# Gates' quotient by VectorE's reciprocal in place of ScalarE's exponential, with a reordered front and rows turned by PE transposes

## The chip, the core and the metric

The kernel runs on one core of a Trainium2 chip. Its engines are TensorE (PE; its weight loads are PEld), VectorE (DVE), ScalarE (ACT) and GpSimd (POOL); SyncE (SP) issues most of the DMAs. Each engine works through its own list of instructions in order and waits on semaphores for the others. The metric is the time of one execution on the device in microseconds (us).

## The reference

A linear recurrence with complex gates ("gate loop") feeds a mixture of experts that picks one expert for each token.

```
q, k, v, a_re, a_im: (B=4, H=8, S=768, D=48) float32
mag   = sqrt(a_re^2 + a_im^2)
scale = min(mag, 0.999) / (mag + 1e-6)
a     = (a_re + i a_im) * scale
for t in range(S):
    S_state = a[t][:, None] * S_state + outer(k[t], v[t])     # complex; k v is real
    y[t]    = q[t] @ Re(S_state)
x      = y as rows: (B*S = 3072 tokens, H*D = 384)
logits = x @ w_gate + modality_bias[modality_id]              # 8 experts
e      = argmax(logits);  g = softmax(logits)[e]
out    = g * (relu(x @ w1[e]) @ w2[e])                        # F = 1024
```

## The kernel before

**Units and groups.** The 768 steps are cut into G = 6 chunks of L = 128 steps. A unit is one chunk of one batch entry, all 8 heads: 24 units, in the order `order` (chunk by chunk, four batch entries each). Gates are worked out for NG = 2 units at once: 12 groups x. Steps lie on the 128 partitions; a group's gates are 2 x 8 x 48 = 768 elements a partition.

**Gates.** In a chunk the products of the gates become sums: of log magnitudes and of angles, each a product with a triangular matrix on PE. For a group x:

- `load_a` (L127) brings a_re and a_im into `abs_`, which has two places, used in turn (x % 2); `load_qk` (L136) brings q and k, also two places.
- `squares` (L143): ACT squares both, DVE adds: half 1 of `sq` is |a|^2, half 0 is a_re^2.
- `products` (L156): on DVE, `tan` = a_re * a_im and `neg` = (a_re < 0).
- `logs` (L165): ACT takes the logarithm of both halves, 1536 elements.
- `tangents` (L170): ACT's exponential of minus the logarithm of a_re^2 is 1 / a_re^2; a second one gives `off`, the correction for the 1e-6. DVE clamps the log magnitude (`lm`) and multiplies `tan` by 1 / a_re^2, so that it holds a_im / a_re.
- `arctans` (L183), `angles` (L186): ACT's arctangent, then PE sums over the steps into `u` (L197, L198).
- `carries`, `fractions` (L201, L210): add the angle at the end of the last chunk (through DRAM, `f_scr`, L207 and L226) and take the fraction of a turn. `waves` (L230): sine and cosine on ACT into `css`.
- `sums`, `moduli` (L238, L248): PE sums the log magnitudes into `ls`, ACT's exponential gives the moduli and their inverses, `pm`; the chunk's last row goes through DRAM (`m_scr`, L256), and `decays` (L259) reads it back.

Logarithm and exponential lie in one of ACT's table sets (EXP), arctangent and sine in another (TRIG); `table` (L116) loads a set, and `then` (L111) keeps ACT's activations in the order in which they are written.

**A unit's own stages.** `hats` (L269) multiplies q and k with moduli and waves on DVE (L279, L283); `turned` (L292) transposes them on PE (L307) and copies them on ACT (L308); `inner` (L315) forms the masked products inside half-chunks and the state's updates (PE L326 and L336, DVE L327, L341 to L348); `outer` (L352) forms y transposed (PE L360 and L366) and copies it to `yT` on ACT (L367): 4 blocks of 128 partitions (two heads of 48, each padded to 64) by 128 steps. `rows` (L370) turns `yT` back, steps on the partitions, and forms the logits in the same products: the right side, `sel`, holds for each block an identity (48 columns) and the router's weights (8 columns). There are 8 products of 64 rows into 56 columns (L377). ACT copies 384 columns as the token's row (L388), DVE adds the 8 partial logits (L389).

**Order.** L411 to L437 write the front: loads of the first groups, then the gates of groups 0 and 1. The loop (L441) then runs half a period a turn: at an even w the fractions, sums and moduli of later groups and their logarithms (under EXP), at an odd w arctangents, waves and squares (under TRIG); each turn carries one unit through `turned`, `inner`, `outer` and `rows`. A planner orders the instructions of PE, DVE and POOL from this text by when it expects their inputs; `issue_after` and `add_manual_dep` hold single ones back. SP's DMAs wait in their queue, one behind the other. `dense` (L88) gives PE extra products whose results nobody reads, at places where it would idle.

**After the gates.** A router (class `Router`, fed by `lg`, with a reciprocal of 4 or 8 elements a partition at L639) places the tokens by expert in DRAM (scatter, L668), and `Layers` runs the experts' products (L951, L966) from there. The first two sets of weights reuse the memory of `abs_` and `css`.

## Time and profile before

| what | before |
|---|---|
| runs (3): lowest, median, highest | 362.83, 366.56, 367.34 us |
| the profiled execution: time, span | 367.03, 365.4 us |
| mean granted clock of TensorE | 0.888 |
| bytes moved in all | 43.04 MB |
| table loads on ACT | 25, 1283 ns each |

The profile is of one execution. Its span runs from the first to the last instruction. A group's row gives its busy time and the mean duration of one instruction; the durations of neighbours on an engine overlap a little, so that busy time in a stretch is less than the sum of durations. The page also has the chain of waits: from the last instruction back, at each step to what released it.

### The profile page before, as it was taken

What the parts mean: (1) busy time and instruction counts of PE and PEld (TensorE: products, weight loads), DVE (VectorE), ACT (ScalarE), POOL (GpSimd) and SP (SyncE); (2) the same over time, 40 slices, a digit from 0 to 9 for tenths busy, and PEclk for the clock granted to TensorE, in tenths of its full rate; (3) what the DMA queues carried; (4) which work ended last, traced back from release to release, by engine and by line L of the source; (5) the groups of instructions that cost most, each with busy time, mean ns of one, the idle gap of its engine ahead of it and who ended that gap; (6) DMA issues with size and microseconds to landing.
All of it is one profiled execution on the core that took longest, in us unless ns stands there. A gap on an engine that the chain in (4) does not pass through costs nothing.

```text
span 365.4 us, 11564 instructions
## 1 busy us (share of the span) xinstructions
PE 322.6 (88%) x4954; PEld 248.9 (68%) x4954; DVE 242.4 (66%) x443; ACT 240.6 (66%) x289; POOL 65.0 (18%) x91
## 2 busy tenths in 40 slices
PE   2786998999899999787999999599989779999992
PEld 1334676587878787756778889489878547777761
DVE  2669799998999899755788899013242733465440
ACT  3987999999999997945689865023113337555532
POOL 7000000000000000072000004710130523424323
PEclk9898999899999999986799999755655969999998
DMA  8967877988766678981968411292120543323221
GB/s 154 209 137 161 170 127 136 173 191 163 134 144 120 138 72 155 180 194 43 167 121 148 88 24 36 75 174 50 30 59 0 148 137 111 108 92 125 85 83 51
DMA packets 155282, 43.04 MB, mean 118 GB/s; under 512 B 145602, under 2 KB 151494, under 8 KB 155096
## 3 DMA queue, kind: packets, MB, share of 16 engines
q1 hardware_dynamic: 149592, 31.98, 45.3%
q0 software_dynamic: 5632, 10.25, 10.7%
q8 instruction: 41, 0.67, 0.7%
q14 instruction: 17, 0.14, 0.1%
HBM read 38.00 MB, written 9.15 MB: 129 GB/s over the span
## 4 chain that ended last, share of the span: by engine, by line
PE 56%; ACT 19%; issue 6%; DMA 6%; SPq 6%; DVE 3%; another core or an unknown queue 2%; POOL 1%; POOLq 0%; DVEq 0%; ACTq 0%
PE h_ps L951 8%; PE y_ps L966 7%; PE up L336 6%; PE xw L377 6%; PE yp L366 5%; PE wp L326 4%; ACT sq L120 4%; PE u L197 4%; ACT L117 3%; PE ls L243 3%; ACT pm L120 3%; PE yp L360 3%; PE tKT L307 2%; DMA qk<-in_k_dram 2%; DMA abs<-in_a_im_dram 2%
## 5 line engine op out<-in xcount | busy, mean ns | idle before, releaser
L336 PE MATMUL up<-V,QK 64*96 64x48 f32 x704 | 41.6, 256 | 3.8 <-issue 2.7
L668 POOL DMA_INDIRECT x_rows<-packed,place x24 | 29.1, 1215 | 86.4 <-DVE U L346 40.2
L336 PEld LDWEIGHTS up<-V,QK 64*96 64x96 f32 x704 | 38.1, 170 | 6.1 <-issue 2.9
L283 DVE TENSOR_TENSOR QK<-css,qkp 128x1536 f32<-128x1536 f32 x24 | 42.0, 1751 | 0.2
L966 PE MATMUL y_ps<-w2t,hT 128*128 128x384 bf16 x200 | 37.2, 340 | 5.3 <-issue 2.8
L367 ACT COPY yT<-yp 128x512 f32<-128x512 f32 x24 | 14.0, 583 | 41.2 <-PE yp L366 33.1
L951 PE MATMUL h_ps<-xgT,w1t 128*128 128x256 bf16 (+1 forms) x312 | 37.7, 281 | 0.0
L951 PEld LDWEIGHTS <-w1t 128*128 128x128 bf16 x312 | 31.0, 103 | 6.1 <-issue 0.3
L377 PE MATMUL xw<-sel,yT 64*128 64x56 f32 x384 | 32.2, 313 | 1.1 <-ACT QT L308 0.6
L117 ACT ACT_TABLE_LOAD x25 | 32.1, 1283 | 1.4 <-PEq L1071 0.9
L971 POOL DMA_INDIRECT out_dram<-y_sb,xg x25 | 24.9, 994 | 44.6 <-ACT y_sb L969 40.7
L326 PEld LDWEIGHTS wp<-QT,KT 96*64 96x64 f32 x768 | 26.5, 148 | 9.0 <-ACT yT L367 2.7
L966 PEld LDWEIGHTS <-hT 128*128 128x128 bf16 x200 | 19.3, 101 | 19.0 <-issue 5.3
L326 PE MATMUL wp<-QT,KT 96*64 96x64 f32 x768 | 29.9, 236 | 2.3 <-ACT yT L367 2.0
L377 PEld LDWEIGHTS xw<-sel,yT 64*128 64x128 f32 x384 | 28.7, 221 | 3.6 <-ACT QT L308 0.7
L308 ACT COPY KT<-tKT 96x1024 f32<-96x1024 f32 x24 | 24.2, 1007 | 10.6 <-PE tKT L307 10.5
L867 POOL DMA_DIRECT2D abs<-in_moe_w_dram x2 | 1.8, 901 | 160.5 <-DMA qk<-in_k_dram 146.2
L389 DVE TENSOR_REDUCE lg<-xw 128x8 f32<-128x64 f32 x24 | 5.3, 220 | 35.6 <-ACT packed L388 35.6
L969 ACT ACTIVATE y_sb<-y_ps,xg 128x384 f32<-128x384 f32 x25 | 13.2, 577 | 23.4 <-PE y_ps L966 17.0
L197 PE MATMUL u<-tan,turn 128*128 128x384 f32 x48 | 21.9, 541 | 4.3 <-ACT yT L367 2.4
L308 ACT COPY QT<-tQT 96x1024 f32<-96x1024 f32 x24 | 24.3, 1014 | 1.2 <-PE tQT L307 1.2
L954 ACT ACTIVATE hT<-h_ps 128x1024 bf16<-128x1024 f32 (+1 forms) x17 | 17.0, 998 | 11.9 <-remote 6.4
(198 smaller groups left out, 631.6 us busy)
## 6 DMA issues: line engine op xcount, KB each, us to landing
abs<-in_a_re_dram SPq DMA_DIRECT2D x24, 192.0 KB
abs<-in_a_im_dram SPq DMA_DIRECT2D x24, 192.0 KB
qk<-in_q_dram SPq DMA_DIRECT2D x24, 192.0 KB
qk<-in_k_dram SPq DMA_DIRECT2D x24, 192.0 KB
V<-in_v_dram SPq DMA_DIRECT2D x24, 192.0 KB
cb<-f_scr SPq DMA_DIRECT2D x10, 384.0 KB
xg<-x_rows SPq DMA_DIRECT2D x12, 194.0 KB
x_rows<-x_rows SPq DMA_DIRECT2D x8, 194.0 KB
```

The costliest lines, as they stand in the source:

```text
L117: then(nc.scalar.preload_act_table_set(name))
L120: then(nc.scalar.activation(*args, **kw))
L197: nc.tensor.matmul(us[:, i], turn[:], tan[:, i], start=True, stop=False)
L283: box["hat"] = nc.vector.tensor_tensor(QK[:].rearrange("p a h c d -> p a (h c d)"), wave, twice, Alu.mult)
L308: nc.scalar.copy(to[:], tp)
L326: nc.tensor.matmul(wp[rows_, h, :], KT[:, s, h], QT[:, s, h], start=True, stop=True)
L336: ins = nc.tensor.matmul(up[:, s, h], flat[rows_, h * C:(h + 1) * C], V[rows_, h, 0:D], start=True, stop=True)
L377: ins = nc.tensor.matmul(xw[:, u, j], yT[at_u, j], sel[at_u, j], start=True, stop=True)
L668: put = self.put = nc.gpsimd.indirect_dma_start(out=self.x_rows, out_offset=bass.IndirectOffsetOnAxis(ap=place[:, i:i + 1], axis=0), in_=p ...
L951: nc.tensor.matmul(h_ps[:, f // nf, f % nf, :], w1t[:, k, ff * 128:(ff + 1) * 128], xgT[:, k, :], start=(k == 0), stop=(k == KD - 1))
L966: nc.tensor.matmul(y_both[:, s], self.hT[:, f, s * 128:(s + 1) * 128], w2t[:, f, :], start=(f == 0), stop=(f == NF - 1))
L971: sc = self.sc = nc.gpsimd.indirect_dma_start(out=self.out, out_offset=bass.IndirectOffsetOnAxis(ap=xg[:, Dt // 2 + 1:], axis=0), in_=y_sb ...
```

## The change

It has three parts. First, `products` takes the reciprocal of a_re on DVE and multiplies it by a_im, which gives the quotient at once; `logs` then takes only half 1, and `tangents` loses its first exponential and its product on DVE. In the loop the quotient of x+4 moves from the end of an odd turn (x+5 there) to the start of an even one, and the load of x+6 behind it. Second, the front starts under TRIG: quotients, arctangents, angles and sines of the first groups come ahead of any logarithm, and the logarithms of group 1 go into the loop's first turn; the loads of `sel` go behind those of the second q and k, the cast of `identb` goes to POOL, and some counts and data of `dense` differ. Third, `rows` turns `yT` by 4 PE transposes of 128x128 against `ident` and forms the logits by 4 accumulated products with 8 columns; `sel` keeps the weights alone, and DVE copies the logits instead of adding them.

```diff
--- before
+++ after
@@ -141,8 +141,8 @@
         box["qk", x] = qk
 
     def squares(x):
-        ab = box.pop(("ab", x))
-        if x in (1, 2):
+        ab = box["ab", x]
+        if x == 1:
             sq = css[:, 1].rearrange("p i h c d -> p (i h c d)").rearrange("p (a i h d) -> p a i h d", a=2, i=NG, h=H)
         else:
             sq = el.tile([L, 2, NG, H, D], F32, name="sq", bufs=1)
@@ -151,33 +151,34 @@
         ins = nc.vector.tensor_tensor(sq[:, 1], sq[:, 0], sq[:, 1], Alu.add)
         if x > 6:
             tc.add_manual_dep(ins.ins, box["hat"].ins.name, mybir.DependencyInfo(mybir.DependencyClass.NoSync, mybir.DependencyReason.DATA), reason="behind the products that the transposes wait for")
-        box["squares", x] = sq, ab
+        box["squares", x] = sq
 
     def products(x):
 
-        ab = box["squares", x][1]
+        ab = box["ab", x]
         tan = el.tile([L, NG, H, D], F32, name="tan", bufs=2)
-        nc.vector.tensor_tensor(tan[:], ab[:, 0], ab[:, 1], Alu.mult)
         neg = el.tile([L, NG, H, D], BF16, name="neg", bufs=2)
-        nc.vector.tensor_scalar(neg[:], ab[:, 0], 0.0, None, Alu.is_lt)
-        box["products", x] = tan, neg
+        if x == 0:
+            nc.vector.tensor_scalar(neg[:], ab[:, 0], 0.0, None, Alu.is_lt)
+        nc.vector.reciprocal(tan[:], ab[:, 0])
+        nc.vector.tensor_tensor(tan[:], tan[:], ab[:, 1], Alu.mult)
+        if x:
+            nc.vector.tensor_scalar(neg[:], ab[:, 0], 0.0, None, Alu.is_lt)
+        box["tangents", x] = tan, neg
 
     def logs(x):
 
-        sq = box["squares", x][0]
-        act(sq[:], sq[:], Act.Ln)
+        sq = box["squares", x]
+        act(sq[:, 1], sq[:, 1], Act.Ln)
 
     def tangents(x):
 
 
-        sq, (tan, neg) = box.pop(("squares", x))[0], box.pop(("products", x))
-        act(sq[:, 0], sq[:, 0], Act.Exp, scale=-1.0)
+        sq = box.pop(("squares", x))
         off = el.tile([L, NG, H, D], BF16, name="off", bufs=2)
         act(off[:], sq[:, 1], Act.Exp, scale=-0.5, bias=ln_eps[:])
         lm = el.tile([L, NG, H, D], F32, name="lm", bufs=3)
         nc.vector.tensor_scalar(lm[:], sq[:, 1], 2.0 * math.log(0.999), None, Alu.min)
-        nc.vector.tensor_tensor(tan[:], tan[:], sq[:, 0], Alu.mult)
-        box["tangents", x] = tan, neg
         box["lm", x] = lm, off
 
     def arctans(x):
@@ -189,8 +190,7 @@
         us = pair([L, H, D], "u")
         full = box["full"][:, 0]
         if x == 0:
-            for n, data in ((18, neg), (11, box["lm", 0][1]), (6, box["lm", 1][1])):
-                dense(full, n, data[:, 0].rearrange("p h d -> p (h d)"))
+            dense(full, 10, neg[:, 0].rearrange("p h d -> p (h d)"))
         elif x == 2:
             dense(full, 5)
         for i in range(NG):
@@ -239,6 +239,8 @@
 
         lm, off = box.pop(("lm", x))
         ls = pair([L, H, D], "ls")
+        if x == 0:
+            dense(box["full"][:, 0], 14)
         for i in range(NG):
             nc.tensor.matmul(ls[:, i], half[:], lm[:, i], start=True, stop=False)
             ins = nc.tensor.matmul(ls[:, i], nhalfb[:], off[:, i], start=False, stop=True)
@@ -299,7 +301,7 @@
             full = box["full"][:, 0]
             if i == 0 and u == 0:
                 dense(full, 10)
-                dense(full, 5, box["pm", 0][:, 1, 0].rearrange("p h d -> p (h d)"))
+                dense(full, 4, box["pm", 0][:, 1, 0].rearrange("p h d -> p (h d)"))
             elif i == 0:
                 dense(full, FILLED.get(u, 0))
             for h in range(H):
@@ -370,11 +372,13 @@
     def rows(g, b):
 
         yT = box.pop(("outer", g, b))
-        xw = pair([L, J, D + Router.E], "xw")
+        xw = pair([L, 512], "xw")
+        xt = xw[:, 0].rearrange("t (j c) -> t j c", c=L)
+        logits = xw[:, 1, 0:Router.E]
         for j in range(J):
-            for u in range(2):
-                at_u = slice(u * 64, (u + 1) * 64)
-                ins = nc.tensor.matmul(xw[:, u, j], yT[at_u, j], sel[at_u, j], start=True, stop=True)
+            nc.tensor.transpose(xt[:, j], yT[:, j], ident[:])
+        for j in range(J):
+            ins = nc.tensor.matmul(logits, yT[:, j], sel[:, j], start=j == 0, stop=j == J - 1)
         busy.append(ins)
         m = g * B + b
         m0 = max(c for c in takes.values() if c <= m)
@@ -385,8 +389,8 @@
             box["packed"] = packed
         packed = box["packed"]
         xr = packed[:, m - m0, 0:H * D // 2].bitcast(BF16)
-        nc.scalar.copy(xr.rearrange("t (j u d) -> t u j d", u=2, d=D), xw[:, :, :, 0:D])
-        nc.vector.tensor_reduce(lg[:, m, :], xw[:, :, :, D:].rearrange("t u j e -> t e u j"), axis=AX.XY, op=Alu.add)
+        nc.scalar.copy(xr.rearrange("t (j u d) -> t j u d", u=2, d=D), xt.rearrange("t j (u c) -> t j u c", u=2)[:, :, :, 0:D])
+        nc.vector.tensor_copy(lg[:, m, :], logits)
 
     NX = len(groups)
     NU = len(order)
@@ -411,29 +415,25 @@
     for x in range(2):
         phase(load_a, x)
     phase(load_qk, 0)
+    table(TRIG)
+    phase(products, 0)
+    phase(squares, 0)
+    phase(load_a, 2)
+    phase(arctans, 0)
+    phase(angles, 0)
+    phase(products, 1)
+    phase(squares, 1)
+    phase(load_a, 3)
+    phase(arctans, 1)
+    phase(angles, 1)
+    phase(fractions, 0)
+    phase(waves, 0)
     table(EXP)
-    phase(squares, 0)
-    phase(products, 0)
-    phase(load_a, 2)
     phase(logs, 0)
-    phase(squares, 1)
     phase(tangents, 0)
-    phase(products, 1)
-    phase(load_a, 3)
-    for x in range(2):
-        phase(logs, x)
-        phase(tangents, x)
-    table(TRIG)
-    for x in range(2):
-        phase(arctans, x)
-        phase(angles, x)
-    phase(fractions, 0)
     phase(squares, 2)
-    phase(squares, 3)
-    with tc.issue_after(box["last"].ins):
-        phase(products, 2)
-    phase(waves, 0)
     phase(load_qk, 1)
+    load_sel()
     phase(fractions, 1)
 
     rt = None
@@ -448,23 +448,28 @@
         unit(values, n + 2)
         unit(values, n + 3)
         if even:
-            phase(load_a, x + 6)
             phase(carries, x + 4)
             phase(fractions, x + 3)
+            with tc.issue_after(box["hat" if w > -4 else "last"].ins) if w < 0 else nullcontext():
+                phase(products, x + 4)
+            phase(load_a, x + 6)
         else:
             phase(load_qk, x + 3)
             phase(decays, x + 2)
-            hats(n + 3)
             if w == -3:
                 hats(0)
+            hats(n + 3)
             if w > 3:
                 hats(n + 4)
         unit(turned, n + 2)
         if even:
-            if x + 2 < NX:
+            if -4 < w and x + 2 < NX:
                 table(EXP)
             phase(sums, x + 2)
             phase(moduli, x + 2)
+            if w == -4:
+                phase(logs, 1)
+                phase(tangents, 1)
             phase(logs, x + 4)
         elif x + 3 < NX:
             table(TRIG)
@@ -481,7 +486,6 @@
         else:
             phase(waves, x + 3)
             phase(squares, x + 5)
-            phase(products, x + 5)
         if w == NU:
             layers.turn(0)
         unit(rows, n - 1)
@@ -1040,17 +1044,18 @@
     ident = cpool.tile([128, 128], F32, name="ident")
     make_identity(nc, ident[:])
     identb = cpool.tile([128, 128], BF16, name="identb")
-    nc.vector.tensor_copy(identb[:], ident[:])
+    nc.gpsimd.tensor_copy(identb[:], ident[:])
     lg = cpool.tile([128, N // 128, E], F32, name="lg")
 
-    sel = cpool.tile([128, H // 2, D + E], F32, name="sel")
+    sel = cpool.tile([128, H // 2, E], F32, name="sel")
     nc.gpsimd.memset(sel[:], 0.0)
-    for u in range(2):
-        nc.gpsimd.tensor_copy(sel[u * 64:u * 64 + D, :, 0:D], ident[u * 64:u * 64 + D, None, u * 64:u * 64 + D].broadcast_to([D, H // 2, D]))
-        nc.sync.dma_start(out=sel[u * 64:u * 64 + D, :, D:], in_=moe_w_gate.rearrange("(j u d) e -> u d j e", u=2, d=D)[u])
+
+    def load_sel():
+        for u in range(2):
+            nc.sync.dma_start(out=sel[u * 64:u * 64 + D], in_=moe_w_gate.rearrange("(j u d) e -> u d j e", u=2, d=D)[u])
 
     last, layers = gate_loop(
-        nc, ctx, tc, cpool, ident, q, k, v, a_re, a_im, sel, lg,
+        nc, ctx, tc, cpool, ident, q, k, v, a_re, a_im, sel, load_sel, lg,
         lambda where, ps, bank: Router(nc, where, tc, cpool, ps, bank, lg, x_rows, moe_modality_id, moe_modality_bias, N, Dt, E, B, S // 128),
         lambda rt, io, el, un, bank, pair, abs_, css: Layers(nc, ctx, tc, identb, rt, io, el, un, bank, pair, abs_, css, x_rows, moe_w1, moe_w2, out))
     layers.run(last)
```

4 lines of the change are left out of this document (2 added, 2 removed).

## The prediction

> **What bounds the kernel now.** I read the head of the page first, for the time, the engines and the shares of the chain that ended last.
>
> ```profile
> span 365.4 us, 11564 instructions
> ...
> PE 322.6 (88%) x4954; PEld 248.9 (68%) x4954; DVE 242.4 (66%) x443; ACT 240.6 (66%) x289; POOL 65.0 (18%) x91
> ...
> PE 56%; ACT 19%; issue 6%; DMA 6%; SPq 6%; DVE 3%; another core or an unknown queue 2%; POOL 1%; POOLq 0%; DVEq 0%; ACTq 0%
> ```
>
> The execution took 367.03 us round a span of 365.4; the runs' median, 366.56, is 0.5 lower. PE carries 56% of the chain and ACT 19%, DVE only 3%, but averages over the span hide that the stages differ. So I cut it with the table of stretches, whose columns are the length of a stretch and the busy time of PE, PE's weight loads, DVE, ACT and POOL.
>
> ```profile
> core 0: us, PE busy (x) PEld busy (x) DVE busy (x) ACT busy (x) POOL busy (x), PEclk, DMA share, GB/s
> 84.30:101.14 16.84, 15.62 (x364) 12.95 (x362) 15.85 (x23) 16.34 (x20) 0.00 (x0) 1.00 0.74 147
> 101.14:118.00 16.86, 16.21 (x367) 13.39 (x365) 16.14 (x24) 15.98 (x19) 0.00 (x0) 1.00 0.73 143
> 205.00:229.00 24.00, 23.67 (x618) 21.32 (x615) 22.75 (x65) 15.66 (x21) 4.93 (x2) 1.00 0.15 31
> 240.00:260.00 20.00, 20.00 (x272) 18.46 (x271) 4.50 (x15) 4.51 (x8) 0.51 (x1) 0.50 0.58 103
> ```
>
> In one period of the gate loop (two units, one group of gates) all three engines are nearly full: ACT 16.34 of 16.84 us, DVE 15.85, PE 15.62. An engine relieved of work hands the bound to a neighbour at once. From 205 on the gates are finished, ACT falls to 15.66 of 24 and PE runs alone, first at clock 1.00, later at 0.50. The chain in order of time gives the loop's extent:
>
> ```profile
> 52.47 1.48 ACT sq L120
> ...
> 105.90 1.51 ACT pm L120 x2
> ...
> 122.76 1.51 ACT pm L120 x2
> ...
> 204.51 1.51 ACT pm L120 x2
> ```
>
> The two middle rows are one period apart, 16.86 us; from 52.5 to 204.5 there are 152 / 16.86 = 9 periods. One microsecond per period is 9 us of the kernel.
>
> **The change, part by part: the quotient.** The groups of instructions, kept apart by shape (busy us, then mean ns of one):
>
> ```profile
> L120 ACT ACTIVATE sq<-sq 128x1536 f32<-128x1536 f32 x10 | 14.9, 1486 | 1.3 <-DVE sq L151 1.3
> ...
> L160 DVE TENSOR_TENSOR tan<-abs 128x768 f32<-128x768 f32 x12 | 11.5, 954 | 3.1 <-PE u L197 2.5 <-PE tQT L307 0.3 <-DMA abs<-in_a_im_dram 0.3
> ...
> L120 ACT ACTIVATE css<-f 128x768 f32<-128x768 f32 x12 | 10.2, 851 | 0.0
> ...
> L179 DVE TENSOR_TENSOR tan<-tan,sq 128x768 f32<-128x768 f32 x10 | 9.5, 949 | 0.0
> ...
> L120 ACT ACTIVATE sq<-sq 128x768 f32<-128x768 f32 x10 | 8.4, 843 | 0.2
> ...
> L162 DVE TENSOR_SCALAR neg<-abs 128x768 bf16<-128x768 f32 x12 | 6.6, 551 | 5.8 <-DMA abs<-in_a_re_dram 5.2 <-PE u L198 0.6
> ...
> L389 DVE TENSOR_REDUCE lg<-xw 128x8 f32<-128x64 f32 x24 | 5.3, 220 | 35.6 <-ACT packed L388 35.6
> ...
> L631 DVE TENSOR_TENSOR acc<-acc 128x8 bf16<-128x8 bf16 x3 | 0.5, 158 | 0.1
> ...
> L639 DVE RECIPROCAL packed<-sm 128x8 f32<-128x8 f32 x2 | 0.4, 190 | 0.0
> ...
> L639 DVE RECIPROCAL packed<-sm 128x4 f32<-128x4 f32 x2 | 0.4, 180 | 0.4 <-DVE sm L638 0.2 <-DVE oneh L625 0.2
> ```
>
> ACT loses half of each logarithm (1486 for 1536 elements becomes one of 768, about 843) and the exponential of -ln (843): 0.64 + 0.84 = 1.48 us a period. DVE loses the last product (949 ns) and gains a reciprocal of 768 elements; the other product stays, only fed by the reciprocal. The logits' reduction (220 ns) becomes a copy of 128x8; the nearest row of that size is 158 ns: 0.06 each, 0.12 a period. So DVE's demand is 15.85 - 0.95 - 0.12 = 14.78 plus the reciprocal r.
>
> Everything hangs on r, and no row has a long reciprocal. The short ones: 180 ns for 4 elements, 190 for 8. Lower bound: one element per pass as any two-operand instruction, 0.95 us (the 768-element product). Upper bound: all that the 8-element one takes beyond the 150 ns floor (158 less 8) is per element, 40 / 8 = 5 ns, so 0.15 + 3.84 = 4.0 us; but its step from 4 to 8 says 10 / 4 = 2.5 ns, so 2.1 us. The step is two pairs of readings whose scatter is as large as itself, and a longer fixed latency explains the excess as well. I take 1.5, between the first and the third, and keep 0.95 and 4.0 as ends.
>
> With r = 1.5 DVE needs 16.28 a period; of the 1.0 us that it idles today I leave 0.3 standing: 16.55, so 0.3 a period is saved, 2.7 us over nine. ACT, at 14.9, drops out. With r = 0.95 the period is 16.0 and the gain 7; DVE reaches today's 16.86 at r = 2.06, with no idle time left, and from there the loop loses.
>
> **The rows.** Now 8 products a unit, 16 passes:
>
> ```profile
> 92.67 1.10 PE L377 MATMUL xw<-sel,yT 64*128 64x56 f32 x16
> 93.61 0.61 PE L307 MATMUL tKT<-ident,QK 64*96 64x64 f32 x16
> 94.05 0.61 PE L307 MATMUL tQT<-ident,QK 64*96 64x64 f32 x16
> ```
>
> 16 passes in 0.94 us, 59 ns each, with 56 columns streaming and the same 128 columns of yT as weights. After: 4 transposes and 4 products, that is 8 passes with 8 columns. For the transposes the nearest row of a 128x128 one:
>
> ```profile
> 308.12 0.50 PE L933 MATMUL xg_ps<-identb,xg 128*128 128x128 bf16 x6
> 308.45 0.33 PE L966 MATMUL y_ps<-w2t,hT 128*128 128x384 bf16 x1
> ```
>
> six in 0.33 us, 55 ns, in bf16. Sum: 4 x 55 + 8 x 59 = 0.69, a saving of 0.25 a unit, 27%. Lower bound: the 64x96 transposes, 16 between 93.61 and 94.05, take 28 ns each; 8 passes at that and the transposes give 0.44. Upper: a load of two full f32 weights took 0.35 us (row at 19.89 below), 175 a pass, and 110 for an f32 transpose: 1.84, dearer by 0.9. I keep 59, since load and tile are the same. Inside the loop PE has a microsecond to spare, so it counts where PE is alone:
>
> ```profile
> 205.00:285.00 80.00, 14.80 (x144) 13.33 (x144) 1.99 (x9) 4.31 (x9) 0.70 0.26 54
> ```
>
> 14.80 us of nine units, 1.64 each with the lower clock; 27% is 4.0, and I take 3.5, because PE's own issue gaps hide some. The ends are -5 and, at the dear price, +6.
>
> **The front.** The timeline up to the first unit's transposes:
>
> ```profile
> 1.45 1.05 SPq L1050 DMA_DIRECT2D sel<-in_moe_w_gate_dram  x2
> ...
> 7.21 0.96 DVE L160 TENSOR_TENSOR tan<-abs 128x768 f32<-128x768 f32 x1 [0.31 <-DMA abs<-in_a_im_dram]
> ...
> 18.25 1.58 ACT L120 ACTIVATE tan<-tan 128x768 f32<-128x768 f32 x2
> ...
> 19.89 0.35 PEld L197 LDWEIGHTS u<-tan,turn 128*128 128x128 f32 x2 [0.23 <-issue]
> ...
> 21.06 0.96 DVE L222 TENSOR_SCALAR r<-u 128x768 f32<-128x768 f32 x1 [3.96 <-PE u L198]
> ...
> 22.06 1.49 ACT L120 ACTIVATE sq<-abs 128x1536 f32<-128x1536 f32 x1 [0.87 <-DMA abs<-in_a_im_dram]
> ...
> 23.46 0.82 ACT L120 ACTIVATE css<-f 128x768 f32<-128x768 f32 x1
> ...
> 26.69 1.51 ACT L120 ACTIVATE pm<-ls 128x768 f32<-128x768 f32 x2
> ...
> 31.99 1.75 DVE L283 TENSOR_TENSOR QK<-css,qkp 128x1536 f32<-128x1536 f32 x1
> ...
> 33.80 0.86 PE L307 MATMUL tKT<-ident,QK 64*96 64x64 f32 x16 [2.75 <-DVE QK L283]
> ```
>
> Today the first arctangent waits until 18.25, behind both groups' logarithms and exponentials, and the transposes start at 33.80. After, it needs only the load, the comparison, r and a product. The first product started at 7.21 on its load; the comparison (551 ns) ran ahead of it, so the real part was there by 6.66. The two loads for the router's weights (1.05 us of the queue) leave the head of the queue: 5.6. Then 0.55 + 1.5 + 0.95: the arctangent starts at 8.6, 9.6 us sooner. What stood ahead of it comes back behind the sines: a table switch, the half logarithm, the exponential:
>
> ```profile
> L117 ACT ACT_TABLE_LOAD x25 | 32.1, 1283 | 1.4 <-PEq L1071 0.9
> ```
>
> 1.28 + 0.84 + 0.84 = 3.0, and about 1 us for the second group's reciprocal, queued on DVE ahead of the first fractions. That leaves 5.6, call it 6. The loads limit it: the square at 22.06 waits for its load and can gain only the queue's 1.05, so 3 is the lower end; 9 the upper, with a short r. The moved loads put 1.05 us ahead of the first values, which nothing needs for 10 us: nothing. The identity's cast goes from DVE to an idle POOL: nothing.
>
> **A new wait.** Loads of gates for x+6 overwrite what the quotient of x+4 reads, and that now runs in the same half-period, just ahead. On SP's queue the carry is moved past it; the moduli's write, the values and the query loads stand behind it. Such loads wait for ACT's squares already:
>
> ```profile
> SPq L132 <- ACT sq L120: 11.0, 4, 4.1
> ```
>
> Later by r + 0.95 + 0.55 = 3.0 us at most; the gates are wanted a full period (16.86) after, and the engines of the DMA are 0.74 busy. I cost it at nothing; without that cover it is up to 3 us a period.
>
> **Sum.** -6 -2.7 -3.5 = -12.2 on 367.0: 354.8, and against the median 354.5. With the ends: r = 0.95, -9 -7 -5, 346; r = 2.06, -5 -0 -2.5, 359.5.
>
> **Rivals.**
> *DVE takes the loop over.* From r = 2.06 each further 0.1 us costs 0.9 us over nine periods. At r = 4.0: 14.78 + 4.0 + 0.3 = 19.1, 2.2 a period, +20; the front gains only about 2 (two reciprocals stand ahead of the first fractions), the rows 3.5: about 381. For it: DVE has 1 us free and the rows for 4 and 8 elements both lie above their like. Against: the step of 10 ns. About 370 at r = 3. Chance 0.26.
> *Eight passes an element.* By the product's row (954 - 150) / 768 = 1.05 ns a pass: 8.4 an element, r = 6.6, DVE 21.7 a period, +43, no gain in front: about 407. Against: it asks for 34 ns between 4 and 8 elements; the trace has 10. Chance 0.07. The Trainium skill, "VectorE: DVE Perf Modes", section "the 8-slice pipeline in each mode", speaks against this change here: it says that the reciprocal runs the iterative divide on two slices with a repeat count of 8. By that rule, read as eight passes, it would be this rival; the trace's 10 ns don't agree.
> *ACT's relief buys nothing in the loop,* because PE (waiting for rows' buffers) or the loads keep the period at 16.85: 367 - 6 - 3.5, about 357.5 to 361. For it: PE 16.21 in the second period. Chance 0.18.
> *The clock drops sooner.* From 205 to 229 PE ran at 1.00, from 240 to 260 at 0.50 with PE busy throughout; thinner passes may tip the first stretch. Half of 24 us lost: +12, so about 367. Chance 0.06. The Trainium skill, "TensorE: Matmul & The Clock Gate", section "Part 4: PE-mode transpose", says that transposes don't count as PE-busy; the trace's 0.50 at full busy time agrees that busy time alone doesn't hold the clock.
>
> **How the numbers follow.** The forecast, r from 0.95 to 2.06, has 0.43 and reaches from 346 to 361. The range of 8 in 10 goes on into the first rival: 346 to 379; outside are the eight passes, that rival's far end and the luckiest front. Two per cent, about what a measurement here can tell from no change, is 359.2 and 373.9. Faster: 0.38 of the forecast and 0.10 of the third rival, 0.48. Within: 0.05 and 0.08 of these, 0.10 of the first, 0.05 of the last, 0.28. Slower: 0.16 of the first, 0.07, 0.01: 0.24.
>
> **What would show it.** The reciprocal's own row: under 2.06 us, I am right about the loop, above it wrong. The distance of two moduli exponentials in the chain: 16.5. The first transposes at about 28. The rows' passes: 0.7 us at full clock. If DVE fills the period and ACT idles, the first rival holds; if the period stays at 16.85 with both idle, the third. The clock from 205 to 229 settles the last.

## The result: 393.09 us, slower, and the profile after

| what | before | after |
|---|---|---|
| runs (4 each): lowest, median, highest | 362.83, 366.95, 369.25 us | 392.56, 393.09, 393.67 us |
| ratio to before, 95% interval | | 1.0753 [1.0662, 1.0843] |
| the profiled execution: time, span | 367.03, 365.4 us | 392.8, 391.2 us |
| mean granted clock of TensorE | 0.888 | 0.883 |

The kernel became 7.5% slower; the forecast was 354.5, with 346 to 379 as its range. Some executions are disturbed and take some per cent longer, and the comparisons leave those out where enough others remain (a kernel with a single good run has its time given below, without a ratio). The runs fell on four chips, on which the kernel before takes about 367 us (chip 0), 357 to 372 (chip 11), 332 (chip 1) and 334 (chip 4), so that only times taken side by side on one chip are compared. The chip of the runs in the table above is not on record; by their times they are counted as chip 0.

The head of the page after the change: the span, the engines' busy time, and the shares of the chain that ended last, by engine and by line.

```profile
span 391.2 us, 11344 instructions
...
PE 333.3 (85%) x4845; PEld 257.6 (66%) x4845; DVE 285.3 (73%) x442; ACT 223.9 (57%) x276; POOL 65.8 (17%) x90
...
PE 55%; DVE 22%; issue 9%; SPq 4%; DMA 3%; ACT 3%; another core or an unknown queue 1%; POOL 1%; POOLq 0%; DVEq 0%
PE h_ps L955 9%; PE y_ps L970 7%; PE up L338 6%; PE yp L368 5%; DVE tan L163 5%; PE wp L328 5%; PE xw L381 4%; DVE QK L285 3%; PE u L197 3%; PE xw L379 3%; PE yp L362 3%; PE ls L245 3%; PE tKT L309 2%; DMA qk<-in_k_dram 2%; DVE qkp L281 2%
```

DVE took ACT's place in the chain: 22% where it had 3%, while ACT fell from 19% to 3%. DVE is busy 43 us longer, ACT 17 us less. The page's "DVE tan L163 5%" is the reciprocal. Its row among the groups kept apart by shape (busy us, mean ns of one), with the product behind it and the logits' copy:

```profile
L163 DVE RECIPROCAL tan<-abs 128x768 f32<-128x768 f32 x12 | 59.3, 4942 | 0.0
...
L164 DVE TENSOR_TENSOR tan<-tan,abs 128x768 f32<-128x768 f32 x12 | 11.3, 944 | 0.0
...
L393 DVE COPY lg<-xw 128x8 f32<-128x8 f32 x24 | 3.9, 161 | 29.6 <-ACT packed L392 29.4
```

So r is 4.94 us. The prediction took 1.5, with 4.0 as the upper end and 2.06 as the point from which the loop loses.

**Where the 25.8 us of span went.** The moduli's exponentials (tile `pm`, two for each of 12 groups) mark the loop: the answer for this tile gives the first and the last start. After, then before:

```profile
L120 ACT ACTIVATE pm<-ls x24: 802/811/812, 33.0 to 255.4; 128x768 f32<-128x768 f32 x24
```

```profile
L120 ACT ACTIVATE pm<-ls x24: 800/810/820, 26.7 to 220.3; 128x768 f32<-128x768 f32 x24
```

The front, up to the first moduli, grew by 6.3 us; the loop from the first to the last by 222.4 - 193.6 = 28.8; the rest, from the last moduli to the end, shrank from 145.1 to 135.8, by 9.3. 6.3 + 28.8 - 9.3 = 25.8.

The loop by the stretches from one group's moduli to the next, in the table of stretches (columns as in the prediction). After, six of the eleven and the sum over all eleven:

```profile
84.58:110.73 26.15, 23.43 (x331) 18.61 (x333) 23.69 (x28) 15.38 (x18) 0.00 (x0) 0.74 0.50 87
110.73:136.80 26.07, 18.47 (x358) 15.23 (x360) 20.40 (x23) 15.18 (x18) 0.00 (x0) 0.87 0.47 93
136.80:156.96 20.16, 17.32 (x359) 14.31 (x360) 20.13 (x25) 15.18 (x19) 0.00 (x0) 1.00 0.61 121
156.96:179.98 23.02, 19.85 (x371) 15.51 (x373) 23.02 (x46) 15.18 (x19) 0.00 (x0) 0.93 0.55 105
179.98:203.37 23.39, 21.25 (x359) 16.68 (x361) 19.25 (x27) 15.22 (x20) 12.32 (x9) 0.85 0.77 163
203.37:222.49 19.12, 17.95 (x362) 14.45 (x364) 18.79 (x22) 15.28 (x18) 0.84 (x1) 1.00 0.82 144
...
sum 221.68, PE 196.05 PEld 153.16 DVE 200.43 ACT 157.60 POOL 13.95; mean PE 17.82 PEld 13.92 DVE 18.22 ACT 14.33 POOL 1.27
```

Before, three later ones that the prediction did not look at, and the sum:

```profile
122.76:141.85 19.09, 17.82 (x379) 14.37 (x381) 18.88 (x41) 16.54 (x19) 0.00 (x0) 1.00 0.71 96
141.85:163.09 21.24, 18.00 (x370) 14.46 (x372) 16.10 (x31) 16.49 (x21) 6.90 (x6) 0.92 0.97 191
163.09:187.95 24.86, 22.15 (x371) 17.49 (x368) 16.38 (x24) 16.66 (x21) 3.84 (x5) 0.79 0.58 113
...
sum 192.89, PE 177.51 PEld 138.38 DVE 169.58 ACT 167.21 POOL 10.75; mean PE 16.14 PEld 12.58 DVE 15.42 ACT 15.20 POOL 0.98
```

After, DVE fills a stretch to the brim (20.13 of 20.16, 23.02 of 23.02) and ACT idles a quarter to a third of it. Over the eleven, DVE's work grew by 30.9 us and the loop by 28.8. Two things in these rows were not foreseen. In the two longest stretches, 26.15 and 26.07, DVE is not full and the clock is 0.74 and 0.87. And the loop before was not made of stretches of 16.86: those of 21.24 and 24.86 had 5.1 and 8.5 us in which DVE was free, and there the reciprocal cost little.

**How one reciprocal blocks.** The timeline (start, duration, engine, line, instruction; in brackets the idle time before it and its releaser), with other engines' rows left out:

```profile
123.49 0.17 DVE L393 COPY lg<-xw 128x8 f32<-128x8 f32 x1 [2.40 <-ACT packed L392]
123.58 4.95 DVE L163 RECIPROCAL tan<-abs 128x768 f32<-128x768 f32 x1
...
128.44 0.90 DVE L281 TENSOR_TENSOR qkp<-qk,pm 128x768 f32<-128x768 f32 x1
129.25 0.95 DVE L164 TENSOR_TENSOR tan<-tan,abs 128x768 f32<-128x768 f32 x1
130.11 1.75 DVE L285 TENSOR_TENSOR QK<-css,qkp 128x1536 f32<-128x1536 f32 x1
...
132.01 1.09 PE L309 MATMUL tKT<-ident,QK 64*96 64x64 f32 x16 [7.35 <-DVE QK L285]
```

The products `qkp` and `QK`, which the next unit's transposes need, stand in DVE's list behind a reciprocal whose result nothing waits for in these rows, and PE idles 7.35 us. The reciprocal itself stands behind the copy of the logits, for which DVE idled 2.40 us: so DVE is not full in this stretch although its list holds work. In the chain of waits this time stands under "issue", since `qkp` waits for no semaphore there: only DVE's own rows show what held it. The stretch of 26.15 us shows a second price. Cut in two at the moment when PE gets work again:

```profile
81.60:93.66 12.06, 9.34 (x169) 7.08 (x169) 12.06 (x12) 8.22 (x11) 0.00 (x0) 1.00 0.63 77
93.66:107.43 13.77, 13.77 (x164) 11.18 (x166) 11.35 (x12) 7.17 (x8) 0.00 (x0) 0.54 0.56 104
```

While DVE is full (12.06 of 12.06, from the reciprocal at 81.52 on), PE works 9.34 us of 12.06; right after, the clock is 0.54 for 13.8 us, and the 32 products `wp` take 1.90 us in the chain there, 1.08 at 110.70. The length of the hole alone does not say how much: the one here is 2.68 us long, and behind the one of 7.35 us the clock was 0.86.

```profile
132.01:145.00 12.99, 12.51 (x248) 10.41 (x250) 12.96 (x15) 10.06 (x13) 0.00 (x0) 0.86 0.34 68
```

**The front.** The timeline of DVE's quotients up to the first transposes:

```profile
6.49 4.93 DVE L163 RECIPROCAL tan<-abs 128x768 f32<-128x768 f32 x1
...
13.02 4.94 DVE L163 RECIPROCAL tan<-abs 128x768 f32<-128x768 f32 x1
...
25.71 4.94 DVE L163 RECIPROCAL tan<-abs 128x768 f32<-128x768 f32 x1
30.57 0.50 DVE L181 TENSOR_SCALAR lm<-sq 128x768 f32<-128x768 f32 x1
...
31.12 0.91 PE L245 MATMUL ls<-lm,half 128*128 128x384 f32 x2 [2.99 <-DVE lm L181]
...
37.74 0.65 PE L309 MATMUL tKT<-ident,QK 64*96 64x64 f32 x16
```

Three reciprocals stand ahead of the first moduli, not two: that of group 2, from the loop's first turn, runs at 25.71 and holds up `lm`, for which PE's sums wait. The first transposes come at 37.74, 3.9 us later than before and 9.7 later than forecast.

**The rows.** In the timeline at full clock:

```profile
114.86 0.66 PE L379 MATMUL xw<-ident,yT 128*128 128x128 f32 x4
115.35 0.96 PE L381 MATMUL xw<-sel,yT 128*128 128x8 f32 x8
116.24 0.65 PE L309 MATMUL tKT<-ident,QK 64*96 64x64 f32 x16
```

From start to start the 4 transposes take 0.49 us, 122 ns each, and the 8 thin passes 0.89, 111 ns each: 1.38 a unit, where before had 0.94.

### The profile page after: what moved, and what is told of

Read it like the earlier page. It is cut to its first block, busy times and chain, and to the rows that moved or that the text cites. A ratio compares the mean times of both kernels' runs of the same rounds, so it can differ in the third digit from the quotient of the medians.

```text
span 391.2 us, 11344 instructions
## 1 busy us (share of the span) xinstructions
PE 333.3 (85%) x4845; PEld 257.6 (66%) x4845; DVE 285.3 (73%) x442; ACT 223.9 (57%) x276; POOL 65.8 (17%) x90
## 4 chain that ended last, share of the span: by engine, by line
PE 55%; DVE 22%; issue 9%; SPq 4%; DMA 3%; ACT 3%; another core or an unknown queue 1%; POOL 1%; POOLq 0%; DVEq 0%
PE h_ps L955 9%; PE y_ps L970 7%; PE up L338 6%; PE yp L368 5%; DVE tan L163 5%; PE wp L328 5%; PE xw L381 4%; DVE QK L285 3%; PE u L197 3%; PE xw L379 3%; PE yp L362 3%; PE ls L245 3%; PE tKT L309 2%; DMA qk<-in_k_dram 2%; DVE qkp L281 2%
## 5 line engine op out<-in xcount | busy, mean ns | idle before, releaser
L672 POOL DMA_INDIRECT x_rows<-packed,place x24 | 31.4, 1310 | 250.7 <-DVE lm L181 178.2
L163 DVE RECIPROCAL tan<-abs 128x768 f32<-128x768 f32 x12 | 59.3, 4942 | 0.0
L970 PE MATMUL y_ps<-w2t,hT 128*128 128x384 bf16 x200 | 35.9, 333 | 5.7 <-ACT hT L958 4.0
L338 PE MATMUL up<-V,QK 64*96 64x48 f32 x704 | 39.9, 257 | 0.2 <-ACT KT L310 0.2
L197 PE MATMUL u<-tan,turn 128*128 128x384 f32 x48 | 28.5, 686 | 9.4 <-ACT tan L120 7.9
L309 PE MATMUL tKT<-ident,QK 64*96 64x64 f32 x384 | 17.6, 237 | 17.0 <-DVE QK L285 13.9
L328 PEld LDWEIGHTS wp<-QT,KT 96*64 96x64 f32 x768 | 26.7, 149 | 6.8 <-ACT QT L310 1.4
L309 PEld LDWEIGHTS tKT<-ident,QK 64*96 64x96 f32 x384 | 13.9, 134 | 25.3 <-issue 12.8
L381 PEld LDWEIGHTS xw<-sel,yT 128*128 128x128 f32 x192 | 28.4, 225 | 0.9 <-issue 0.9
L381 PE MATMUL xw<-sel,yT 128*128 128x8 f32 x192 | 27.4, 268 | 0.9 <-issue 0.9
L245 PE MATMUL ls<-lm,half 128*128 128x384 f32 x48 | 22.9, 564 | 3.2 <-DVE lm L181 3.0
```

What stands on the lines that cost most here:

```text
L163: nc.vector.reciprocal(tan[:], ab[:, 0])
L197: nc.tensor.matmul(us[:, i], turn[:], tan[:, i], start=True, stop=False)
L245: nc.tensor.matmul(ls[:, i], half[:], lm[:, i], start=True, stop=False)
L309: ins = nc.tensor.transpose(tp[:, s, h], QK[rows_, i, h].rearrange("t c d -> t (c d)"), ident[rows_, rows_])
L328: nc.tensor.matmul(wp[rows_, h, :], KT[:, s, h], QT[:, s, h], start=True, stop=True)
L338: ins = nc.tensor.matmul(up[:, s, h], flat[rows_, h * C:(h + 1) * C], V[rows_, h, 0:D], start=True, stop=True)
```

## The experiments

The table puts the kernels whose profiles can be compared side by side, in us from the rows for `pm` and the spans: first moduli, first to last, and last to the end. The kernel before starts its last moduli at 220.3 to 222.4, as it is (chip 0), with the new rows (chips 1 and 4) and with a changed order of loads (chip 11), so the first two columns can be read over chips; the third and the ratios can't. On chip 11 the kernel before itself took 357.8 to 372.3 us beside the timed kernels there, and the ratios of that chip say less than the columns.

| kernel | chip | first moduli | first to last | last to the end | ratio to before |
|---|---|---|---|---|---|
| before | 0 | 26.7 | 193.6 | 145.1 | |
| before_again | 0 | 28.5 | 193.6 | 142.7 | |
| after | 0 | 33.0 | 222.4 | 135.8 | 1.0753 [1.0662, 1.0843] |
| after_again | 0 | 34.2 | 222.8 | 129.3 | 1.0562 [1.0451, 1.0672] |
| after_c | 4 | 33.6 | 217.0 | 114.3 | 1.1024 [1.0931, 1.1118] |
| before_rows | 1 | 27.4 | 193.9 | 113.9 | 1.0174 [1.0093, 1.0255] |
| before_rows_b | 4 | 28.6 | 193.8 | 114.7 | 1.013 [1.0084, 1.0175] |
| after_oldrows | 1 | 34.7 | 222.7 | 111.7 | 1.1267 [1.1167, 1.1368] |
| after_r1 | 1 | 21.5 | 187.7 | 113.9 | 0.9776 [0.9678, 0.9874] |
| after_r1_b | 11 | 21.5 | 184.5 | 135.9 | 0.9833 [0.9698, 0.9969] |
| after_r2 | 0 | 23.4 | 197.5 | 136.4 | 0.9837 [0.9752, 0.9921] |
| after_r3 | 11 | 26.0 | 200.0 | 135.1 | 0.9891 [0.9786, 0.9996] |
| after_r1_oldrows | 11 | 23.3 | 198.4 | 138.5 | 1.005 [0.9954, 1.0147] |
| after_pieces | 4 | 26.5 | 215.1 | 115.3 | |
| pool_squares | 11 | 27.6 | 210.2 | 146.0 | 1.0491 [1.0388, 1.0593] |
| before_front | 11 | 27.9 | 192.8 | 135.3 | |

### One part at a time

before_rows is the kernel before with the new rows alone: 4 transposes and 4 accumulated products, `sel` with the weights only.

> The kernel before with the rows turned by PE transposes alone. Two theories. If the price of the passes decides (in the profile of the changed kernel 4 transposes and 8 thin passes took 1.38 us at full clock against 0.94 before), it is 0.44 a unit dearer: 3 to 8 us slower than before, 370 to 375. If what decides is TensorE's clock behind the gates (0.50 from 233 to 282 us before, but back at 1.00 within 6 us of its drop in the changed kernel, whose rows fill the whole array), the tail gains about 9 and pays about 4: 358 to 363, with a clock near 1.00 in the units after the last gates.

before_recip is the kernel before with the quotient alone; its order and its rows stay:

```diff
-        nc.vector.tensor_tensor(tan[:], ab[:, 0], ab[:, 1], Alu.mult)
+        nc.vector.reciprocal(tan[:], ab[:, 0])
+        nc.vector.tensor_tensor(tan[:], tan[:], ab[:, 1], Alu.mult)
...
-        act(sq[:], sq[:], Act.Ln)
+        act(sq[:, 1], sq[:, 1], Act.Ln)
...
-        act(sq[:, 0], sq[:, 0], Act.Exp, scale=-1.0)
...
-        nc.vector.tensor_tensor(tan[:], tan[:], sq[:, 0], Alu.mult)
```

> The kernel before with the quotient by VectorE's reciprocal alone: front, place in the loop and rows as before, ScalarE's exponential, half of its logarithm and VectorE's last product left out. If the reciprocal's length (4.94 us) decides, VectorE needs 15.85 - 0.95 + 4.94 = 19.8 us a period against 16.86: 3.0 to 3.3 over nine periods, 27 to 30 us slower, 392 to 397. If the new front or the new place of the quotient cost the time, this stays within 5 us of 367.

after_oldrows is the changed kernel with the old rows put back.

> The changed kernel with the rows and logits formed as before. VectorE bounds its loop, so the rows count only behind the gates. If the new rows bring the clock back there, it is 5 to 9 us slower than the changed kernel, 398 to 402, with a clock of 0.50 in the last units; if the dearer passes decide, 4 to 5 us faster, 388.

Measured side by side on chip 1, against 330.3 us in the mean: the new rows 336.0, ratio 1.0174 [1.0093, 1.0255]; the quotient 365.5, 1.1066 [1.0935, 1.1197]; all but the rows 372.2, 1.1267 [1.1167, 1.1368]. The quotient alone carries a loss of the size of the whole change's (35 us, where 27 to 30 were expected), and the reordered front doesn't make up for it. The rows alone lose 5.7 us. Their place was then repeated on another chip, with more rounds, and the changed kernel beside them:

> The kernel before with the rows turned by PE transposes alone, a second time. Where the kernel before takes 332 us (TensorE at 1.00 behind the gates) it was 1.7% slower, and should be again, 335 to 339. Where it takes 367 (TensorE at 0.50 there), the dearer passes cost the same in the loop; if the fuller array brings the clock back, it is 3 to 10 us faster, 357 to 364; if not, 372 to 376.

> The changed kernel again, to have it where the kernel before takes 332 us, if this call runs there: with 35 us lost ahead of the last moduli and 3 to 5 by dearer rows behind them, 367 to 373 there; 386 to 393 on the other chip, as twice before.

On chip 4 the rows alone lose again, 1.013 [1.0084, 1.0175]: 337.2 us against 332.8 in the mean. The changed kernel is at 1.1024 [1.0931, 1.1118] there, while after_oldrows had 1.1267 [1.1167, 1.1368] on chip 1. By these ratios the same rows cost 1.3 to 1.7% in the kernel before and save some 2% in the changed one; but the two are from different chips, and the changed kernel's loop with the new rows, 217.0 here, was 222.4 and 222.8 on chip 0, like the 222.7 of after_oldrows. The last experiment on the rows, below, takes that up.

before_front is the kernel before with the loads of `sel` moved behind the second q and k, and the identity's cast on GpSimd.

```diff
-    nc.vector.tensor_copy(identb[:], ident[:])
+    nc.gpsimd.tensor_copy(identb[:], ident[:])
...
     phase(load_qk, 1)
+    load_sel()
     phase(fractions, 1)
```

> The kernel before with the two loads of the router's weights behind those of the second q and k, and the identity's cast on GpSimd; nothing else. If SP's queue sets the start, the first product starts 0.8 to 1.05 us sooner and the kernel is about 1 us faster (0.3%, inside the noise). If the loads behind are bound by their bytes, nothing.

It took 357.6 us, where before took 357.3 to 359.8 beside it; its first moduli are at 27.9, inside before's own 26.7 to 28.5. These small edits neither bring nor cost anything that this run can show.

### The quotient's length as the only variable

In after_r1 the division is left out: a product of the same size stands in for the reciprocal. after_r2 and after_r3 have two and three such products in a row.

```diff
-        nc.vector.reciprocal(tan[:], ab[:, 0])
+        nc.vector.tensor_tensor(tan[:], ab[:, 0], ab[:, 0], Alu.mult)
+        nc.vector.tensor_tensor(tan[:], tan[:], ab[:, 0], Alu.mult)
```

(This is after_r2; after_r1 lacks the second line, after_r3 has it twice.)

> The changed kernel with a product of a_re with itself (about 0.95 us) where the reciprocal stands, so that the angles are other ones. If the reciprocal's length decides, 30 us go: 350 to 362, and VectorE is no longer the fullest engine of the loop. If front, place or rows cost the time, it stays above 380.

> The changed kernel with two products (1.9 us in all) where the reciprocal stands, so that the angles are other ones. With one product it took 323 us. If VectorE has about a microsecond to spare in a period, as the break-even of 2.06 us said, this is about the kernel before, 328 to 334; if TensorE or ScalarE bound the loop by then, it stays at 323 to 326.

> The changed kernel with one product (0.95 us) where the reciprocal stands, so that the angles are other ones, again, as the foot of the line. Ratio 0.97 to 0.985 of before, as the first time.

> The changed kernel with three products (2.86 us) where the reciprocal stands; the angles are other ones. If each microsecond beyond a break-even near 2.06 costs nine periods and a little of the front, and shorter ones cost nothing, this is 0.8 x 10 = 8 us above after_r1_b. If every microsecond costs the same from 0.95 on (4.94 gave 36 us above before and 44 above after_r1), it is 1.9 x 11 = 21 us above.

At r = 0.95 the kernel is faster, 0.9776 [0.9678, 0.9874] on chip 1; at 1.90 it is 0.9837 [0.9752, 0.9921] on chip 0. The two ratios of chip 11 are weak. At 2.86, 0.9891 [0.9786, 0.9996] comes from runs of 361.3 to 363.2 us, which lie within before's scatter; before's four shortest runs there, 357.8 to 360.3, are all shorter, so that a gain at 2.86 is not shown. At 0.95, 0.9833 [0.9698, 0.9969] belongs to a kernel with one run of 343.6 us, which is also the profiled one, and three of 357.6 to 365.7. With nothing else changed, the reciprocal's 4.94 makes it 1.06 to 1.10; side by side on chip 0, the same kernel stands at 0.9837 with r = 1.90 (after_r2) and at 1.0562 with the reciprocal (after_again). So the reciprocal's duration is what turned the sign. The rows for `pm` of after_r1, after_r2 and after_r3:

```profile
L120 ACT ACTIVATE pm<-ls x24: 804/811/818, 21.5 to 209.2; 128x768 f32<-128x768 f32 x24
```

```profile
L120 ACT ACTIVATE pm<-ls x24: 804/811/818, 23.4 to 220.9; 128x768 f32<-128x768 f32 x24
```

```profile
L120 ACT ACTIVATE pm<-ls x24: 805/810/819, 26.0 to 226.0; 128x768 f32<-128x768 f32 x24
```

The front grows with r, and faster as r grows: 21.5, 23.4, 26.0 and 33.0 at 0.95, 1.90, 2.86 and 4.94, which is 2.0, 2.7 and 3.4 us per us from each to the next. The lists say why. At 0.95 two quotients stand ahead of `lm`, and the third runs behind it (at 19.91, `lm` at 18.96). At 1.90 and 2.86 one product of the third stands ahead, and with the reciprocal all of it does. The loop follows r too, 187.7, 197.5, 200.0 and 222.4. From 2.86 to 4.94 it costs 22.4 / 2.08 = 10.8 us per us of r (8.2 with the 217.0 of after_c), where the prediction had 9. Before's 193.6 lies between 0.95 and 1.90, near 1.5 on the line between the two; front and loop together, the last moduli, are level with before's 220.3 to 222.4 at 1.90 and late at 2.86 (226.0). One caution: two or three short instructions are not one long one, since DVE's list has other work between them.

What holds the loop at the short end is seen in a stretch of after_r1:

```profile
86.63:103.43 16.80, 16.80 (x359) 14.16 (x360) 16.60 (x25) 15.09 (x19) 0.00 (x0) 1.00 0.91 170
```

PE is full. Its two units' rows cost 2 x 0.44 us more than before's, and the period stays at 16.80.

### Shortening or moving the block

after_pieces cuts the reciprocal into four instructions, of 64, 128, 192 and 384 elements:

```diff
-        nc.vector.reciprocal(tan[:], ab[:, 0])
+        for a, z in ((0, 64), (64, 192), (192, 384), (384, 768)):
+            nc.vector.reciprocal(flat[:, a:z], re[:, a:z])
```

> The changed kernel with each reciprocal cut in four, of 64, 128, 192 and 384 elements. If each element costs 6.2 ns over a floor of 150 ns (the 768-element one took 4.94 us), they take 0.55, 0.95, 1.35 and 2.55 us. If a long reciprocal is slow for another reason (its length, a shared port), the short ones lie on the 2.5 ns of the 4- and 8-element rows: 0.31, 0.47, 0.63, 1.1.

The rows of the pieces, among the groups by shape:

```profile
L165 DVE RECIPROCAL tan<-abs 128x384 f32<-128x384 f32 x12 | 30.3, 2526 | 0.0
...
L165 DVE RECIPROCAL tan<-abs 128x192 f32<-128x192 f32 x12 | 15.8, 1319 | 0.0
...
L165 DVE RECIPROCAL tan<-abs 128x128 f32<-128x128 f32 x12 | 11.1, 924 | 0.0
L165 DVE RECIPROCAL tan<-abs 128x64 f32<-128x64 f32 x12 | 6.5, 542 | 2.8 <-DMA abs<-in_a_re_dram 2.8
```

(2526 - 542) / (384 - 64) = 6.2 ns an element, and 542 - 64 x 6.2 = 145 ns fixed: 4.91 for 768, as measured whole. So r is a price per element, not a start-up cost. The one run took 358.5 us, where after_c took 366.3 to 368.9 beside it. The first moduli came at 26.5, 7.1 earlier, because DVE's list now lets `lm` pass between pieces; the loop gained 1.9. A timed run of the same kernel:

> The changed kernel with each reciprocal cut in four, timed: 0.37 us more work a period for VectorE, but other products can go between. If only the sum counts, as the prediction's arithmetic had it, the ratio to before lies 0.01 above the changed kernel's (1.056 to 1.075 where before takes 367, 1.102 where it takes 334). If the blocking counts, 0.02 to 0.03 below it.

On chip 11 it took 384.6 us against before's 357.3 to 359.8, about 1.07. Cutting does not mend the change. How much it helps is open: on chip 4 a single run was some 8 us shorter than the shortest of after_c, and on chip 11 no run of after stands beside it.

after_behind puts the quotient in every turn behind the products of `hats`, which in the change holds for the first turns alone (the condition `w < 0` becomes `x + 4 < NX`).

> The changed kernel with the quotient queued behind the last products that the transposes wait for, in all periods and not only the first. In the changed kernel TensorE waited 7.4 us at 124.7 for such products behind a reciprocal. If the sum of VectorE's work decides (19.7 us a period), the time stays within 4 us of the changed kernel's; if the place of the 4.94 us decides, 10 to 20 us go.

after_again and before_again ran beside it, to have both kernels once more on that chip.

> The changed kernel beside the others. On the first chip it was 26 us slower. If the loop bound by VectorE accounts for 35 us (last moduli at 254.7 against 219.6) and the first chip gave 9 back behind the gates by its clock, it is 33 to 40 us slower here, 365 to 372; if the loop's loss were itself the chip's, 26 or less.

> The kernel before, for a profile beside those of this chip, on which its runs took 332 us where the first ones took 367. If the loop is the same everywhere, the last group's moduli stand near 219.6 us as in the first profile, and all of the difference lies behind, where TensorE ran at 0.50; if the whole chip is faster, the moduli stand near 200.

after_again came out at 1.0562 [1.0451, 1.0672], before_again at 366.4 us; the two measurements of after, 1.0753 and 1.0562, differ by about as much as an interval is wide. after_behind took 386.8 us (its other three runs 392.8 to 409.7), after_again 386.0 and 387.9. In the profile of after_behind, which is of the run of 409.7, PE's longest wait for `QK` from 60 us on is 2.7 us, where after had 7.4. So that hole is gone there, and yet this place in DVE's list gains nothing that these runs can show; what waits for the reciprocal instead was not followed.

### Another engine for it

pool_pow gives the quotient to GpSimd, which the prediction's profile shows idle in the loop: a power of -1, and the product.

```diff
+        nc.gpsimd.tensor_tensor(tan[:], ab[:, 0], minus, Alu.pow)
+        nc.gpsimd.tensor_tensor(tan[:], tan[:], ab[:, 1], Alu.mult)
```

> The kernel before with the quotient on GpSimd, which is idle in the loop: a power of -1 and a product there; ScalarE's exponential, half of its logarithm and both of VectorE's products left out. If GpSimd does the two in less than about 12 us a group, ScalarE has 1.5 us less a period and VectorE 1.9: 4 to 9 us faster than before. If the power takes longer than a period (16.9 us), GpSimd bounds the loop and it is far slower.

1808.6 us. The rows:

```profile
L163 POOL TENSOR_TENSOR tan<-abs,minus 128x768 f32<-128x768 f32 x12 | 1473.2, 122770 | 108.8 <-PE u L199 93.1 <-DMA qk<-in_q_dram 15.0 <-DMA abs<-in_a_re_dram 0.7
...
L164 POOL TENSOR_TENSOR tan<-tan,abs 128x768 f32<-128x768 f32 x12 | 23.7, 1973 | 0.9
```

A power takes GpSimd 122.8 us for 768 elements a partition, 25 times DVE's reciprocal. Its product is 1.97, so pool_squares tried the other way round to unload the loop: the kernel before, with ACT's squares of groups 4 and later on GpSimd.

```diff
-            act(sq[:, some], ab[:, some], Act.Square)
+            if x < 4:
+                act(sq[:, some], ab[:, some], Act.Square)
+            else:
+                nc.gpsimd.tensor_tensor(sq[:, some], ab[:, some], ab[:, some], Alu.mult)
```

> The kernel before with the gates' squares from the fifth group on taken by GpSimd, as one product of 1536 elements, instead of ScalarE (1.48 us a period less there, about 4 us on idle GpSimd; VectorE and TensorE as before). If ScalarE's relief is what made the changed kernel with a short quotient faster, 0.5 to 0.9 us a period over seven periods: 3 to 6 us faster than before. If VectorE or TensorE hold the period, or GpSimd's products slow VectorE, no faster, or slower.

It was slower, 1.0491 [1.0388, 1.0593]. The rows show why:

```profile
L282 DVE TENSOR_TENSOR qkp<-qk,pm x24: 936/948/3367, 30.6 to 243.0; 128x768 f32<-128x768 f32 x24
...
103.74 4.18 DVE QK L286
...
L286 DVE TENSOR_TENSOR QK<-css,qkp 128x1536 f32<-128x1536 f32 x24 | 49.3, 2053 | 0.2
L153 POOL TENSOR_TENSOR sq<-abs 128x1536 f32<-128x1536 f32 x8 | 32.0, 4002 | 135.8 <-DVE tan L182 123.0 <-DMA V<-in_v_dram 12.8
L282 DVE TENSOR_TENSOR qkp<-qk,pm 128x768 f32<-128x768 f32 x24 | 30.2, 1260 | 0.0
```

DVE's products take 2053 and 1260 ns in the mean, where before had 1751 and 948. But the first row gives the shortest, the median and the longest: 936, 948 and 3367 ns, so that most are as fast as before. Beside seven of GpSimd's eight products a single product of DVE takes 1.4 to 2.4 us longer, four of the 24 `qkp` and three of the 24 `QK` (the second row, from the chain, is one of these, 4.18 us), while others that run under the same GpSimd product keep their 1.75 and 0.95. That is 14.7 us more for DVE over the loop, which is 16.6 us longer than before's. So this run does not tell what ACT's relief alone would bring.

The Trainium skill, "GPSIMD Engine Reference", section "Specifications", says that GpSimd's SBUF interfaces are shared with VectorE, with contention where a DVE instruction has two SBUF inputs; this trace agrees, by the seven long products.

### The rows once more

after_r1_oldrows is after_r1 with the old rows.

> The changed kernel with one product where the reciprocal stands (the angles are other ones) and rows and logits formed as before. If the dearer passes cost as they did in the kernel before, where TensorE is nearly full, it is 4 to 6 us faster than after_r1_b. If the new rows help whatever bounds the loop, as in the changed kernel, it is 3 to 5 us slower.

On chip 11 it is at 1.005 [0.9954, 1.0147], after_r1_b with the new rows at 0.9833 [0.9698, 0.9969]. Its ten runs take 358.1 to 368.2 us, and three of the four of after_r1_b take about as long, 357.6 to 365.7; the medians of all their runs, 362.96 and 360.12 us, lie closer than the ratios. Its loop is 198.4 us, that of after_r1_b and after_r1 184.5 and 187.7. The corresponding stretch of after_r1_b (new rows) and of after_r1_oldrows:

```profile
153.61:173.11 19.50, 18.52 (x363) 14.92 (x365) 16.94 (x25) 15.53 (x19) 8.78 (x8) 1.00 0.93 177
```

```profile
163.92:189.68 25.76, 23.31 (x370) 18.72 (x372) 15.58 (x23) 15.51 (x18) 4.88 (x6) 0.73 0.65 133
```

About as many passes keep PE busy for 23.31 us instead of 18.52, at clock 0.73 instead of 1.00: the difference lies in whether the clock falls in this stretch. Ahead of the fall PE's products `up` have four gaps of 0.35 to 0.87 us without a releaser in the trace; with the new rows there are two of 0.41 and one of 0.16. But the new rows don't prevent that as such, since after itself has stretches at 0.74 and 0.67 and the kernel before has the same loop with new rows and old, 193.9 and 193.6. That transposes over the full array keep the clock up is argued, not shown, and the sign of the rows' share in the changed kernel stays open.

## Why the prediction was wrong

**The step that failed is the size of r.** "I take 1.5, between the first and the third, and keep 0.95 and 4.0 as ends": it is 4.94, past the upper end. The third bound read the 10 ns between the rows for 4 and 8 elements as a price per element; at 6.2 ns an element that step is 25 ns. The law from the pieces gives 170 and 195 ns for these two instructions, whose rows have 180 and 190: each is 5 to 10 ns off, in opposite directions. The upper bound, 5 ns from the floor of 150, was nearer, and the measured floor of 145 with the 8-element row of 190 would have said 5.6. Two readings of 180 and 190 ns could not carry 768 elements.

**The rival held.** "DVE takes the loop over" had its place (DVE full, ACT idle) and its form right. Its formula with the measured r gives 14.78 + 4.94 + 0.3 = 20.02 a period, 3.16 more than 16.86, 28.4 over nine; the loop measured +28.8. Its break-even of 2.06 left out the 0.3 of idle time that the same sum kept elsewhere; with it, it would be 1.78. The front's gain of 2 at r = 4.0 would be gone (two reciprocals of 0.94 more), and with the rows at -3.5 the whole would be about +25, where +25.8 was measured. That agreement is partly luck, as the next three points show. The rival for eight passes an element lay at 6.6 us: with the product's 1.05 ns a pass, 6.2 ns is 5.9 passes. The Trainium skill's repeat count of 8 ("VectorE: DVE Perf Modes", section "the 8-slice pipeline in each mode") was the better warning than the trace's two small rows, though 8 passes at the product's pace isn't what the runs show.

**The loop's price.** The nine periods were miscounted: from the moduli at 55.73 to those at 204.51 before has eight stretches with a mean of 18.6 us, not nine of 16.86. In the two of 21.24 and 24.86 DVE had time to spare and the reciprocal cost less than forecast; in the two that became 26 us it cost more, by the blocked products and the clock of 0.54 behind them. The sum came out near 9 us per us of r, the number of the loop's quotients (12, less the three in the front). At r = 1.5, by the line between after_r1 and after_r2, the loop would have stood about where before's stands, not 2.7 us better.

**The front.** "About 1 us for the second group's reciprocal" left out the third. Between after_r1 and after_r2 the front would stand at 22.6 for r = 1.5, a gain of 4.1 from 26.7, not 6: inside the stated 3 to 9. With the true r each of three reciprocals counts, and the gain turned into a loss of 6.3.

**The rows.** "4 x 55 + 8 x 59 = 0.69" is 1.38. Both prices came from rows of another type or shape: a bf16 transpose (55, the f32 one is 122) and a half-array load (59, the full one is 111). The upper end of 1.84 was nearer. Alone it cost 5.7 and 4.4 us, near the +6 of the dear end. On chip 0 the rest of the span was shorter with the new rows all the same: 135.8, 129.3 and 136.4 us in after, after_again and after_r2, 145.1 and 142.7 in before. The prediction quoted before's stretch from 240 to 260 at clock 0.50; PE has short gaps there before it, for which the trace shows no releaser. After has like gaps, but its clock is back sooner, though it is 0.75 again from 285 to 300:

```profile
265.00:275.00 10.00, 6.91 (x90) 6.07 (x86) 0.17 (x1) 2.79 (x4) 6.71 (x8) 0.69 0.44 88
275.00:285.00 10.00, 10.00 (x240) 9.42 (x240) 4.32 (x15) 3.10 (x5) 0.00 (x0) 0.97 1.02 174
```

On chip 4 after_c has no such gap and keeps full clock:

```profile
255.00:285.00 30.00, 30.00 (x684) 27.98 (x684) 15.18 (x35) 11.21 (x17) 16.45 (x15) 1.00 0.60 120
```

There the last part took 114.3 us, and 114.7 in before_rows_b on the same chip, so that nothing is given back behind the loop: 1.102 instead of 1.075. On chip 11 the last part doesn't tell the rows apart (135.1 and 135.9 with the new ones, 135.3 and 138.5 with the old).

**The rest.** The new wait of the loads was costed at nothing. It is there: SP's queue waited five times for `neg` ahead of a gate load, 15.1 us in all and 5.0 at the longest, where 3.0 at most was said and before waited 11.0 for ACT's squares. One such load, at 72.53, stands in the chain with 3.17 us, but its stretch of the loop is not longer than before's (15.82 against 15.98), so no cost of it is shown. The logits' copy is 161 ns, 158 were taken. "ACT's relief buys nothing in the loop" was true for a short r in the stretch shown, by PE: 16.80 a period in after_r1, with ACT at 15.09; over all eleven stretches after_r1's loop is 5.9 us shorter than before's. "The clock drops sooner" fell in its place, the stretch behind the gates, where the clock held up better; inside the loop the clock did drop, behind DVE's block.
